# Sums of group 0's w2 made at the end of round one, y's splits ended there too, and last outputs sent by quarters

## The chip, the core and the metric

The kernel runs on one core of a Trainium2 chip. That core has a matmul engine (TensorE, PE in the rows; its weight loads are PEld), a vector engine (VectorE, DVE), a scalar engine (ScalarE, ACT), a general one (GpSimd, POOL) and a synchronising engine (SyncE, SP) that issues most of the DMAs. Each engine works through its own queue in order; semaphores order the engines among themselves. The metric is the device time of one execution in microseconds, as the median of several runs.

## The reference

Three stages follow each other, all in float32:

```python
a = softmax(scale * q_c @ k_full.T)         # 24 chunks of 32 queries; 8 memory keys + a window of 56
x = (a @ v_full) as [1536, 512]             # 1536 tokens
x = (sigmoid(x @ w_gate) * (x @ w_val)) @ w_out
p = probs / (probs.sum(-1) + 1e-9)
for e in range(4):                          # 4 experts, w1[e] is 512x1024, w2[e] 1024x512
    out += p[:, e:e+1] * (relu(x @ w1[e]) @ w2[e])
```

## The kernel before

The change lies wholly in the third stage, the mixture of four experts. Every float32 product is made of three matmuls: each operand is split into a high part (ACT, a cast) and a low part (DVE, the difference), and `mm3` (L181 to L183) multiplies high by high, high by low and low by high.

The four experts are cut into eight *groups* of 512 hidden columns. Tokens are cut into two halves of 768. **Round one** runs blocks 0 to 7, one group each, over the first half; **round two** runs blocks 8 to 15, the groups in reverse order, over the second half. Within a block, the product with w1 is made by a scheme of seven products instead of eight (products 1 to 7 into PSUM tiles `b`, `e` and `a`, in two units `u`, each 384 tokens wide), whose operands are sums and differences of quarters of w1 and of y, the stage's input. The product with w2 is plain in round one (`o_part`, PSUM tiles `d`, added into `acc` by `flush`, L819), and by the seven-product scheme again in round two, so that round two also needs sums of w2's quarters.

What is split or summed in round one is written to DRAM and read back in round two: `kept1` holds w1's seven operands of each group, `kept2` those of w2. `w1_prep(n)` loads and splits w1 of group n, `w2_prep(n)` splits w2 of group n into `w2` tiles and stores three operands (L296), `w2_sums(n)` makes the other four from the raw tiles in place (combinations L311, casts L316, low parts L322, store L324). The last group, 7, is not stored: round two begins with it. The raw w2 tiles come from a pool of two buffers, which are the two tiles of one group; `raw2_to` loads the next group (L223), and that load must wait until the buffers have been read for the last time. `yr` holds y, `yo` its seven split operands; `y_prep_late(1)` makes those of the second half, once block 7's last products have read the old ones.

The order of the work is written by hand. A block's preparations for the next one are lists of closures, `hooks`: `o_part` emits one of them after every three matmuls, the last two are kept back (`keep=2`) and emitted in the next block's first unit behind its first copy `s`. A second list, `thooks`, holds `w2_sums(n)` of blocks 1 to 7 and is emitted in the units. In block 0 the hooks were `w1_prep(1)` (9), `w2_sums(0)` (6) and `w2_prep(1)` (5). In block 7 they were `y_prep_late(1)` (8), of which two were left for round two (`hook(len(hooks))` behind product 6 of block 8). PSUM has eight banks, handed out in turn, so that a tile waits for the one allocated eight before it. `held` (L755) copies a product out of PSUM on ACT into `s`; `total` (L453 in round two) adds it to a later product on DVE.

In the last block, 15, the results of `stage` and `second` go to `st` tiles and are added into `acc` by DMAs of POOL (L524), except for the quarter (second half of the rows, second half of the columns), which DVE adds directly; then `acc` leaves in rows of 512 columns, three transfers from `second` (L518) and three from `c12` (L532).

Of the kernel before, what the change touches and what calls it, by code (L numbers as in the profile page):

```python
# [45 lines left out]
DH = DM // 2  # L46
# [26 lines left out]
def fused_kernel(ctx: ExitStack, tc: tile.TileContext, kq0, kq1, kvw, kvc, vl, w_g, w_v, w_o, w_1, w_2, probs, out):  # L73
# [144 lines left out]
    def raw2_to(n):  # L218
        for i in range(len(raw2s), min(n, len(groups))):
            raw2s[i] = []  # L220
            for fh in range(2):
                r = pools["raw2"].tile([128, 2, DM], F32, tag="raw2", name=f"raw2_{i}_{fh}")
                nc.sync.dma_start(out=r, in_=w_2[groups[i][0], groups[i][1], fh])  # L223
                raw2s[i].append(r)
# [56 lines left out]
    def w2_prep(n):  # L281
        def hi(u, fh):
            def do():
                raw2_to(n + 1)
                w = pools["wp2"].tile([128, 2, DM], F32R, tag="w2", name=f"w2_{n}_{u}_{fh}")
                ops2[n, u, fh] = w
                nc.scalar.copy(out=w[:, 0], in_=raw2s[n][fh][:, u])  # L287
            return do

        def lo(u, fh):  # L290
            def do():
                w = ops2[n, u, fh]
                nc.vector.tensor_tensor(out=w[:, 1], in0=raw2s[n][fh][:, u], in1=f32(w[:, 0]), op=ALU.subtract)  # L293
                if n < NSP:
                    for d in range(2) if fh else range(1):
                        nc.sync.dma_start(  # L296
                            out=kept2[n][:, d + 1 if fh else 0, u], in_=f32(w[:, :, d * DH:(d + 1) * DH]))
            return do


        h, l = ([fn(u, fh) for u in range(2) for fh in range(2)] for fn in (hi, lo))
        return [both(h[0], h[1], l[0]), both(h[2], l[1]), l[2], h[3], l[3]]

    def w2_sums(n):

        r0, r1 = raw2s[n]
        b = dict(b11=r0[:, :, :DH], b12=r0[:, :, DH:], b21=r1[:, :, :DH], b22=r1[:, :, DH:])
# [5 lines left out]
        def hi(m, x):  # L313
            def do():
                w = ops3[n][m] = wp.tile([128, 2, 2, DH], F32R, tag="w", name=f"w3_{n}_{m}")
                nc.scalar.copy(out=w[:, :, 0], in_=b[x])  # L316
            return do

        def lo(m, x):
# [10 lines left out]
            both(lo(7, "b12"), hi(6, "b22"), comb("b21", "b21", "b22", ALU.add)),  # L330
            both(lo(6, "b22"), hi(4, "b21")), both(lo(4, "b21"), lambda: raw2_to(n + 2))]

# [65 lines left out]

    def round_2(prev, hook, hooks, hp, sp, acc, held, product):

# [103 lines left out]
        firsts = {}  # L504

        def stage(n, th, tt, dh, ps):
            p, a, _ = of(n, th, tt, dh)
            if n == ends and (th, dh) == (1, 1):
                nc.vector.scalar_tensor_tensor(out=a, in0=ps[:, :DH], scalar=p, in1=a, op0=ALU.mult, op1=ALU.add)
                return  # L510
# [3 lines left out]
        def second(n, th, tt, dh, ps):  # L514
            p, a, t = of(n, th, tt, dh)
            if n == ends and (th, dh) == (1, 1):
                nc.vector.scalar_tensor_tensor(out=a, in0=ps[:, :DH], scalar=p, in1=a, op0=ALU.mult, op1=ALU.add)
                nc.sync.dma_start(out=out[(RT + t) * 128:(RT + t + 1) * 128], in_=acc[t])  # L518
                return
# [3 lines left out]
            if n > NR1:  # L523
                nc.gpsimd.dma_start(out=a, in_=st, accum_op=ALU.add)  # L524

        def c12(n, tt, ps):
# [3 lines left out]
            elif n == ends:  # L530
                nc.vector.scalar_tensor_tensor(out=a, in0=ps[:, :DH], scalar=p, in1=a, op0=ALU.mult, op1=ALU.add)
                nc.sync.dma_start(out=out[(RT + t) * 128:(RT + t + 1) * 128], in_=acc[t])  # L532
            else:
# [10 lines left out]
        for n in range(NR1, len(blocks)):  # L544
# [21 lines left out]
            s2 = held(b)  # L566
            hook(len(hooks))
            do("6")
# [6 lines left out]
            if late:  # L575
                left["4"](E2)
                load_w3(n, 6)
            lo(n, 0, 1, c11, True)
            product(n, 0, 5, b, False)
            total(b, s7, c22)  # L580
            hi(n, 0, 4, c22, True)
            do("5")
            lo(n, 0, 4, c22, True)
            product(n, 0, 4, e, False)
            total(e, s2, c21)
            hi(n, 0, 2, c21, True)
            do("3_2")
            lo(n, 0, 2, c21, True)
# [114 lines left out]

            if last:
                for tt in tts:
                    third(tt)
# [5 lines left out]
    def second_block():  # L712
# [45 lines left out]
        def unit(n, u, prev):  # L758
# [4 lines left out]
            if u == 0 and n:  # L763
                hook(len(hooks))
                thooks.extend(w2_sums(n))
            if u:
# [38 lines left out]
        def o_part(n, d, tt, u, first, last, cols):  # L805
            th, c = divmod(tt, RT // 2)
            c = slice(c * 128, (c + 1) * 128)
            for fh in range(2):
                h, w = H2[n, u, (fh, th)], ops2[n, u, fh]
                mm3(d[:, cols], h[:, 0, c], h[:, 1, c], w[:, 0, cols], w[:, 1, cols],  # L810
                    first and fh == 0, last and fh == 1)
                hook(keep=2)

# [12 lines left out]
        for n in range(NR1):  # L826
# [10 lines left out]
            if n == NR1 - 1:  # L837
                hooks.extend(y_prep_late(1))
            else:
                hooks.extend(w1_prep(n + 1))  # L840
                if n == 0:
                    hooks.extend(w2_sums(0))
                hooks.extend(w2_prep(n + 1))
            ds = {}
# [24 lines left out]
            part(5, 0)  # L869
            flushed(4)  # L870

            def prev(n=n, ds=ds):
                o_part(n, ds[5], 5, 1, False, True, ALL)
                flush(n, ds[5], 5, ALL)

        round_2(prev, hook, hooks, hp, sp, acc, held, product)
        pools["yo"].release()
# [432 lines left out]
```

## Time and profile before

| what | value |
|---|---|
| median of 3 runs | 855.52 us (854.46 to 857.11) |
| the profiled execution | 854.76 us, of which the span is 852.5 us |
| granted clock of TensorE, mean | 0.995 |
| busy: PE, PEld, DVE, ACT, POOL | 98%, 89%, 60%, 46%, 10% of the span |
| moved by DMA | 167.66 MB, mean 197 GB/s |

The span runs from the first to the last instruction on the chip; the profiled execution's own time is 2.3 us longer. PE's busy share counts matmuls whose ends are modelled and that overlap each other, so it does not say how well PE is used; where PE stood still is read from the waits. Round one starts at about 345 us, round two at about 605 us. In the chain of work that ended last, PE holds 93% of the span, DMA and DVE 2% each.

### The profile page before, as it was taken

What the parts mean: (1) busy time and instruction counts of PE and PEld (TensorE: products, weight loads), DVE (VectorE), ACT (ScalarE), POOL (GpSimd) and SP (SyncE); (2) the same over time, 40 slices, a digit from 0 to 9 for tenths busy, and PEclk for the clock granted to TensorE, in tenths of its full rate; (3) what the DMA queues carried; (4) which work ended last, traced back from release to release, by engine and by line L of the source; (5) the groups of instructions that cost most, each with busy time, mean ns of one, the idle gap of its engine ahead of it and who ended that gap; (6) DMA issues with size and microseconds to landing.
All of it is one profiled execution on the core that took longest, in us unless ns stands there. A gap on an engine that the chain in (4) does not pass through costs nothing.

```text
span 852.5 us, 13705 instructions
## 1 busy us (share of the span) xinstructions
PE 834.3 (98%) x5246; PEld 756.7 (89%) x5246; DVE 514.4 (60%) x963; ACT 392.7 (46%) x835; POOL 88.0 (10%) x101
## 2 busy tenths in 40 slices
PE   9999999999999999978999999999999999999997
PEld 6899998888888888867889989989899999999997
DVE  7754346432342238458997787788467556646756
ACT  5765354322332344525355445346255445545542
POOL 2311000000000000000000000000001343243232
PEclk9999999999999999998999999999999999999999
DMA  8974134121120004594977987730397999999974
GB/s 313 365 271 157 33 125 140 50 75 50 50 75 1 1 0 168 178 342 187 359 265 282 342 292 267 286 142 2 103 357 225 245 305 327 300 277 292 342 167 112
DMA packets 62338, 167.66 MB, mean 197 GB/s; under 512 B 6577, under 2 KB 27329, under 8 KB 62273
## 3 DMA queue, kind: packets, MB, share of 16 engines
q1 hardware_dynamic: 51008, 156.54, 51.1%
q0 software_dynamic: 11264, 10.25, 7.9%
q8 instruction: 41, 0.67, 0.3%
q14 instruction: 25, 0.20, 0.1%
HBM read 102.01 MB, written 54.53 MB: 184 GB/s over the span
## 4 chain that ended last, share of the span: by engine, by line
PE 93%; DMA 2%; DVE 2%; ACT 1%; issue 0%; SPq 0%; POOL 0%; ACTq 0%; DVEq 0%
PE b L181 5%; PE b L182 5%; PE b L183 5%; PE d L183 5%; PE d L182 5%; PE d L181 4%; PE pv L181 4%; PE pv L183 4%; PE pv L182 4%; PE pg L183 4%; PE pg L182 4%; PE pb L182 4%; PE pb L183 4%; PE pb L181 4%; PE pg L181 4%; PE B L183 3%
## 5 line engine op out<-in xcount | busy, mean ns | idle before, releaser
L524 POOL DMA_DIRECT2D acc<-st x60 | 52.4, 970 | 687.7 <-DVE st L522 682.7
L181 PE MATMUL b<-yo,w 128*128 128x384 f32 x256 | 87.9, 343 | 10.3 <-ACT s L755 9.0
L182 PE MATMUL b<-yo,w 128*128 128x384 f32 x256 | 86.8, 339 | 0.0
L183 PE MATMUL b<-yo,w 128*128 128x384 f32 x256 | 86.7, 339 | 0.0
L755 ACT COPY s<-b 128x384 f32<-128x384 f32 x64 | 30.6, 478 | 94.1 <-PE b L183 93.9
L181 PE MATMUL pv<-xs,w_v 128*128 128x384 f32 (+1 forms) x176 | 64.2, 365 | 0.0
L183 PE MATMUL pv<-xs,w_v 128*128 128x384 f32 (+1 forms) x176 | 61.8, 351 | 0.4 <-POOL w_v L161 0.4
L182 PE MATMUL pv<-xs,w_v 128*128 128x384 f32 (+1 forms) x176 | 61.5, 349 | 0.0
L181 PEld LDWEIGHTS b<-yo,w 128*128 128x128 f32 x256 | 48.4, 189 | 14.3 <-ACT s L755 11.6
L1052 ACT ACTIVATE sg<-pg 128x512 f32<-128x512 f32 x36 | 21.5, 598 | 84.2 <-PE pg L183 84.2
L183 PE MATMUL pg<-xs,w_g 128*128 128x512 f32 x144 | 56.0, 389 | 0.0
L182 PE MATMUL pg<-xs,w_g 128*128 128x512 f32 x144 | 56.0, 389 | 0.0
L181 PE MATMUL pb<-hl,w_o 128*128 128x512 f32 x144 | 56.0, 389 | 0.0
L182 PE MATMUL pb<-hl,w_o 128*128 128x512 f32 x144 | 56.0, 389 | 0.0
L183 PE MATMUL pb<-hl,w_o 128*128 128x512 f32 x144 | 56.0, 389 | 0.0
L181 PE MATMUL pg<-xs,w_g 128*128 128x512 f32 x144 | 56.0, 389 | 0.0
L120 DVE TENSOR_TENSOR hl<-g,hl 128x512 fp32r<-128x512 f32 x36 | 24.7, 690 | 48.5 <-ACT hl L119 48.5
L182 PEld LDWEIGHTS b<-yo,w 128*128 128x128 f32 x256 | 48.4, 189 | 1.0
L183 PEld LDWEIGHTS b<-yo,w 128*128 128x128 f32 x256 | 48.3, 189 | 0.0
L119 ACT CAST hl<-g 128x512 fp32r<-128x512 f32 x36 | 22.2, 623 | 54.8 <-PE pb L183 54.8
L181 PE MATMUL e<-yo,w 128*128 128x384 f32 x128 | 43.2, 338 | 0.2 <-ACT st L535 0.2
L293 DVE TENSOR_TENSOR w<-raw,w 128x512 fp32r<-128x512 f32 x32 | 21.2, 687 | 36.7 <-ACT w L287 28.4
(757 smaller groups left out, 2310.9 us busy)
## 6 DMA issues: line engine op xcount, KB each, us to landing
kept<-w SPq DMA_DIRECT2D x77, 512.0 KB, 6.8
w<-kept SPq DMA_DIRECT2D x49, 512.0 KB, 9.5
w_ring<-kept SPq DMA_DIRECT2D x38, 512.0 KB, 6.6
raw<-in_w_dram SPq DMA_DIRECT2D x32, 512.0 KB, 6.6
kept<-w SPq DMA_DIRECT2D x42, 256.0 KB, 6.8
acc<-st POOLq DMA_DIRECT2D x78, 128.0 KB, 5.3
kv<-in_kvc_dram SPq DMA_DIRECT2D x20, 483.0 KB, 5.9
raw<-in_w_v_dram SPq DMA_DIRECT2D x12, 512.0 KB, 6.7
```

Of the source, the lines that this page charges most:

```text
L119: nc.scalar.copy(out=hi, in_=src)
L120: nc.vector.tensor_tensor(out=lo, in0=src, in1=f32(hi), op=ALU.subtract)
L181: nc.tensor.matmul(out=ps, lhsT=w_hi, rhs=r_hi, start=first, stop=False, skip_group_check=more)
L182: nc.tensor.matmul(out=ps, lhsT=w_hi, rhs=r_lo, start=False, stop=False, skip_group_check=more)
L183: nc.tensor.matmul(out=ps, lhsT=w_lo, rhs=r_hi, start=False, stop=last, skip_group_check=more)
L293: nc.vector.tensor_tensor(out=w[:, 1], in0=raw2s[n][fh][:, u], in1=f32(w[:, 0]), op=ALU.subtract)
L524: nc.gpsimd.dma_start(out=a, in_=st, accum_op=ALU.add)
L755: nc.scalar.copy(out=s, in_=ps[:, :HT])
L1052: nc.scalar.activation(out=sg, in_=ps, func=AF.Sigmoid)
```

## The change

Five edits. `raw2_to(2)` is called behind the last low part of `w2_prep(0)`, so that group 1's raw w2 is loaded there. Block 0's hooks no longer hold `w2_sums(0)`. Instead `raw2_to` can load a ninth pair of tiles, `raw2_8`, which is group 0 once more; the load is called at the end of `w2_sums(7)`, and block 7's hooks are `y_prep_late(1)` and `w2_sums(0)` from those tiles, with `keep` 0, so that nothing is left for round two. The four operands of `w2_sums(0)` then come from the pool `rawp` instead of `wp`. In the first unit of each block of round two `lo` of a product stands behind the next `total`. In block 15 both column halves of the second half of the rows are added by DVE (no staging on ACT, no POOL DMA), and every output leaves by itself as 128 rows of 256 columns (`put_out`): those of the second half as soon as each is summed, those of the first columns of the first half (`late_out`, added by POOL) behind them, then the last three.

```diff
     def raw2_to(n):
-        for i in range(len(raw2s), min(n, len(groups))):
+        for i in range(len(raw2s), min(n, NR1 + 1)):
+            g = groups[i % NR1]
...
-                nc.sync.dma_start(out=r, in_=w_2[groups[i][0], groups[i][1], fh])
+                nc.sync.dma_start(out=r, in_=w_2[g[0], g[1], fh])
...
                 nc.vector.tensor_tensor(out=w[:, 1], in0=raw2s[n][fh][:, u], in1=f32(w[:, 0]), op=ALU.subtract)
+                if n == 0 and (u, fh) == (1, 1):
+                    raw2_to(2)
...
-    def w2_sums(n):
-
-        r0, r1 = raw2s[n]
+    def w2_sums(n, at, pool, tag):
+
+        r0, r1 = raw2s[at]
...
-                w = ops3[n][m] = wp.tile([128, 2, 2, DH], F32R, tag="w", name=f"w3_{n}_{m}")
+                w = ops3[n][m] = pool.tile([128, 2, 2, DH], F32R, tag=tag, name=f"w3_{n}_{m}")
...
-            both(lo(6, "b22"), hi(4, "b21")), both(lo(4, "b21"), lambda: raw2_to(n + 2))]
+            both(lo(6, "b22"), hi(4, "b21")), both(lo(4, "b21"), lambda: raw2_to(at + 2))]
...
+        def put_out(t, dh, a):
+            nc.sync.dma_start(out=out[(RT + t) * 128:(RT + t + 1) * 128, dh * DH:(dh + 1) * DH], in_=a)
+
         def stage(n, th, tt, dh, ps):
             p, a, _ = of(n, th, tt, dh)
-            if n == ends and (th, dh) == (1, 1):
+            if n == ends and th:
...
         def second(n, th, tt, dh, ps):
             p, a, t = of(n, th, tt, dh)
-            if n == ends and (th, dh) == (1, 1):
+            if n == ends and th:
                 nc.vector.scalar_tensor_tensor(out=a, in0=ps[:, :DH], scalar=p, in1=a, op0=ALU.mult, op1=ALU.add)
-                nc.sync.dma_start(out=out[(RT + t) * 128:(RT + t + 1) * 128], in_=acc[t])
+                put_out(t, dh, a)
                 return
...
+            if n == ends:
+                late_out.append((t, dh, a))
...
             s2 = held(b)
-            hook(len(hooks))
             do("6")
...
-            lo(n, 0, 1, c11, True)
             product(n, 0, 5, b, False)
             total(b, s7, c22)
             hi(n, 0, 4, c22, True)
+            lo(n, 0, 1, c11, True)
             do("5")
-            lo(n, 0, 4, c22, True)
             product(n, 0, 4, e, False)
             total(e, s2, c21)
             hi(n, 0, 2, c21, True)
+            lo(n, 0, 4, c22, True)
...
             if last:
+                for args in late_out:
+                    put_out(*args)
                 for tt in tts:
                     third(tt)
...
-                thooks.extend(w2_sums(n))
+                thooks.extend(w2_sums(n, n, wp, "w"))
...
-                hook(keep=2)
+                hook(keep=2 if n < NR1 - 1 else 0)
...
-                hooks.extend(y_prep_late(1))
+                hooks.extend(y_prep_late(1) + w2_sums(0, NR1, rawp, "raw"))
             else:
-                hooks.extend(w1_prep(n + 1))
-                if n == 0:
-                    hooks.extend(w2_sums(0))
-                hooks.extend(w2_prep(n + 1))
+                hooks.extend(w1_prep(n + 1) + w2_prep(n + 1))
...
+            if n == NR1 - 1:
+                hook(len(hooks))
```

PE's matmuls keep their order. The places that move are on SP and DVE. In the rows below `raw2_1_0` and `raw2_1_1` are the raw w2 tiles of group 1, `w3_0_5` and the like the summed operands of group 0.

SP in block 0, before:

```order
L215 DMA raw1_3_1_3547<-in_w_1_dram 128x1024
L324 DMA kept2_0_85<-w3_0_5_3556 128x1024
L324 DMA kept2_0_85<-w3_0_7_3564 128x1024
L324 DMA kept2_0_85<-w3_0_6_3573 128x1024
L324 DMA kept2_0_85<-w3_0_4_3581 128x1024
L223 DMA raw2_1_0_3589<-in_w_2_dram 128x1024
L223 DMA raw2_1_1_3591<-in_w_2_dram 128x1024
```

SP in block 0, now:

```order
L299 DMA kept2_0_85<-w2_0_0_1_3361 128x2x256 x2
L299 DMA kept2_0_85<-w2_0_1_0_3392 128x2x256
L224 DMA raw2_1_0_3444<-in_w_2_dram 128x1024
L224 DMA raw2_1_1_3446<-in_w_2_dram 128x1024
L299 DMA kept2_0_85<-w2_0_1_1_3399 128x2x256 x2
L266 DMA kept1_1_79<-w1_1_4_3481 128x1024
```

The load of `raw2_1` moved from behind the four stores of group 0's sums to the stores of group 0's splits, ahead of all seven `kept1` stores of group 1; the stores of the sums are gone from here.

DVE from the end of block 7 to the first sums of block 8, before (`yo3` to `yo6` are y operands, `d7_0` to `d7_5` the PSUM tiles that `flush` reads, `c0` and `c2` the sums of block 8):

```order
L230 TENSOR_TENSOR yo4_2866<-yr0_2859,yo4_2866 128x768
L819 SCALAR_TENSOR_TENSOR acc0_3316<-d7_0_5572,p_sb_75,acc0_3316 128x512
L819 SCALAR_TENSOR_TENSOR acc1_3317<-d7_1_5582,p_sb_75,acc1_3317 128x512
L819 SCALAR_TENSOR_TENSOR acc2_3318<-d7_2_5602,p_sb_75,acc2_3318 128x512
L819 SCALAR_TENSOR_TENSOR acc3_3319<-d7_3_5613,p_sb_75,acc3_3319 128x512
L819 SCALAR_TENSOR_TENSOR acc4_3320<-d7_4_5650,p_sb_75,acc4_3320 128x512
L819 SCALAR_TENSOR_TENSOR acc5_3321<-d7_5_5665,p_sb_75,acc5_3321 128x512
L230 TENSOR_TENSOR yo5_2867<-yr0_2859,yo5_2867 128x768
L230 TENSOR_TENSOR yo3_2868<-yr1_2860,yo3_2868 128x768
L453 TENSOR_TENSOR c0_5684<-a8_0_5731,s_5701 128x384
```

DVE from the same y split on, now (the flushes of `d7_1` to `d7_5`, left out here, and then the sums `c0` and `c2` follow):

```order
L231 TENSOR_TENSOR yo4_2866<-yr0_2859,yo4_2866 128x768
L231 TENSOR_TENSOR yo5_2867<-yr0_2859,yo5_2867 128x768
L231 TENSOR_TENSOR yo3_2868<-yr1_2860,yo3_2868 128x768
L314 TENSOR_TENSOR raw2_8_0_5552<-raw2_8_0_5552 128x2x256
L314 TENSOR_TENSOR raw2_8_0_5552<-raw2_8_1_5554,raw2_8_0_5552 128x2x256
L325 TENSOR_TENSOR w3_0_5_5614<-raw2_8_0_5552,w3_0_5_5614 128x2x256
L314 TENSOR_TENSOR raw2_8_1_5554<-raw2_8_0_5552,raw2_8_1_5554 128x2x256
L325 TENSOR_TENSOR w3_0_7_5622<-raw2_8_0_5552,w3_0_7_5622 128x2x256
L314 TENSOR_TENSOR raw2_8_1_5554<-raw2_8_1_5554 128x2x256
L830 SCALAR_TENSOR_TENSOR acc0_3316<-d7_0_5556,p_sb_75,acc0_3316 128x512
L325 TENSOR_TENSOR w3_0_6_5630<-raw2_8_1_5554,w3_0_6_5630 128x2x256
L325 TENSOR_TENSOR w3_0_4_5640<-raw2_8_1_5554,w3_0_4_5640 128x2x256
```

The two y splits moved from behind the sixth flush to before the first, and the eight instructions of `w2_sums(0)` stand around the first flush.

## Rows read from the trace of the kernel before

**Rows 1.** Waits of PE, 300 to 430 us: who waited for whom, total, times, longest.

```profile
PE b L181 <- ACT s L755: 9.0, 2, 8.3
```

**Rows 2.** Chain of work that ended last, 366 to 395 us: start, length, what.

```profile
375.45 0.94 SPq L223
376.44 9.26 DMA raw<-in_w_dram
...
386.24 0.61 ACT w L287
386.85 0.39 ACT s L755
387.28 0.69 PE b L181
```

**Rows 3.** Timeline of PE, first matmuls of blocks 1, 2, 3: start, length, what.

```profile
375.36 0.33 PE L181 MATMUL b<-yo,w 128*128 128x384 f32 x1
...
416.75 0.33 PE L181 MATMUL b<-yo,w 128*128 128x384 f32 x1
...
448.07 0.33 PE L181 MATMUL b<-yo,w 128*128 128x384 f32 x1
```

**Rows 4.** Stretch 385 to 390: busy PE, PEld, DVE, ACT, POOL; granted clock; DMA share, GB/s.

```profile
385.00:390.00 5.00, 2.72 (x8) 2.72 (x9) 4.89 (x8) 2.89 (x7) 0.00 (x0) 0.50 0.58 195
```

**Rows 5.** Timeline of DVE in block 0.

```profile
356.17 0.68 DVE L293 TENSOR_TENSOR w<-raw,w 128x512 fp32r<-128x512 f32 x1
...
368.65 0.69 DVE L311 TENSOR_TENSOR raw<-raw 128x512 f32<-128x512 f32 x1
```

**Rows 6.** Timeline at the seam, DVE, ACT and PE; in brackets idle time before, releaser.

```profile
590.87 0.68 DVE L322 TENSOR_TENSOR w<-raw,w 128x512 fp32r<-128x512 f32 x1
...
594.55 1.82 DVE L230 TENSOR_TENSOR yo<-yr,yo 128x768 fp32r<-128x768 f32 x2
...
606.06 0.48 ACT L755 COPY s<-b 128x384 f32<-128x384 f32 x1 [10.93 <-PE b L183]
...
608.44 0.76 DVE L819 SCALAR_TENSOR_TENSOR acc<-d,p_sb,acc 128x512 f32<-128x512 f32 x1 [4.10 <-PE d L183]
...
610.72 0.96 DVE L230 TENSOR_TENSOR yo<-yr,yo 128x768 fp32r<-128x768 f32 x1 [0.67 <-ACT yo L227]
...
611.60 0.55 DVE L453 TENSOR_TENSOR c<-a,s 128x384 f32<-128x384 f32 x1
...
612.09 0.34 PE L182 MATMUL e<-yo,w 128*128 128x384 f32 x1
...
612.26 0.34 PE L183 MATMUL e<-yo,w 128*128 128x384 f32 x1
...
613.28 0.55 DVE L453 TENSOR_TENSOR c<-b,s 128x384 f32<-128x384 f32 x1
...
613.98 0.41 PE L181 MATMUL b<-yo,w 128*128 128x384 f32 x1 [1.37 <-DVE c L453]
```

**Rows 7.** Line L223, the 16 loads of raw w2.

```profile
DMA to landing us min/median/max: 5.0/6.4/9.3
```

**Rows 8.** Timeline of the tail, DVE and SP's issues.

```profile
844.44 0.48 DVE L517 SCALAR_TENSOR_TENSOR acc<-B,p_sb,acc 128x256 f32<-128x256 f32 x1 [0.23 <-PE B L183]
...
846.60 0.48 DVE L531 SCALAR_TENSOR_TENSOR acc<-B,p_sb,acc 128x256 f32<-128x256 f32 x1 [0.23 <-PE B L183]
...
846.81 1.37 SPq L532 DMA_DIRECT2D out_dram<-acc  x3
```

**Rows 9.** Landing of outputs: line L532 (the last three), then L821 (round one's).

```profile
DMA to landing us min/median/max: 2.8/3.4/3.5
...
DMA to landing us min/median/max: 2.0/2.0/2.3
```

**Rows 10.** Stretches with `kept2` stores alone, then with POOL's additions; columns as in rows 4.

```profile
355.00:360.00 5.00, 5.00 (x28) 4.87 (x29) 3.52 (x8) 2.19 (x5) 0.00 (x0) 1.00 0.75 262
...
843.00:844.00 1.00, 1.00 (x10) 1.00 (x9) 0.97 (x3) 0.00 (x0) 1.00 (x2) 1.00 0.92 131
```

More of the change, by code (lines that the diff above doesn't have):

```diff
@@ L397, in emit, with round_2 @@
             todo.pop(0)()
-    def round_2(prev, hook, hooks, hp, sp, acc, held, product):
+    def round_2(prev, hp, sp, acc, held, product):
         h_op = [hp.tile([128, 2, HT], F32R, tag="h", name=f"h2_{i}") for i in range(8)]
@@ L524, in second @@
                 nc.gpsimd.dma_start(out=a, in_=st, accum_op=ALU.add)
+            if n == ends:
+                late_out.append((t, dh, a))
+        late_out = []
         def c12(n, tt, ps):
@@ L531, in c12 @@
                 nc.vector.scalar_tensor_tensor(out=a, in0=ps[:, :DH], scalar=p, in1=a, op0=ALU.mult, op1=ALU.add)
-                nc.sync.dma_start(out=out[(RT + t) * 128:(RT + t + 1) * 128], in_=acc[t])
+                put_out(t, 1, a)
             else:
@@ L874, in prev @@
                 flush(n, ds[5], 5, ALL)
-        round_2(prev, hook, hooks, hp, sp, acc, held, product)
+        round_2(prev, hp, sp, acc, held, product)
         pools["yo"].release()
```

## The prediction, made before the result was known

> **What bounds the kernel now.** The program is one long stream of matmuls, so I read first the waits of TensorE (PE): who made it stand still, and for how long. One entry stands out [rows 1]: 9.0 us in two waits behind ScalarE's copy `s` (L755), 8.3 us of it in one piece. That so little else is listed says that PE is the bound nearly everywhere, and that work taken from ACT or DVE beside the matmuls is worth nothing by itself. A gain must come from this wait, from the seam of the two rounds, or from the tail behind the last matmul.
>
> *The long wait.* The chain of waits [rows 2], read backward from PE at 387.28, goes to ACT's copy `s`, to ACT's cast of w2 of group 1 (L287), to the DMA that brings `raw2_1` (9.26 us), to its issue on SP at 375.45. It was issued so late because the pool of raw w2 tiles holds one group: group 1 can be loaded only when group 0's tiles have been read for the last time, by the `w2_sums(0)` that block 0 makes behind `w1_prep(1)`. ACT takes its queue in order, so `s`, which needs nothing of w2, stood behind the cast. Cost: the first matmuls of blocks 1, 2 and 3 start at 375.36, 416.75 and 448.07 [rows 3]. Block 1 took 41.39 us, block 2 31.32. The difference, 10.07 us, holds the wait and the slow stretch behind it: in 385 to 390 the granted clock was 0.50, the lower of the two levels (1.2 GHz), after PE had stood still for 8.3 us [rows 4].
>
> *The seam.* Between 596.37 (594.55 + 1.82) and 608.44 DVE has only flushes to do, and the one at 608.44 even waited 4.10 us for PE; yet two y splits were kept for round two [rows 6]. The last of them, at 610.72, holds the sum `c` of `a` until 611.60 and that of `b` until 613.28. Product 3, which adds to `b`, starts at 613.98, 1.72 us after the matmul before it, where neighbours (612.09, 612.26) are 0.17 apart. Loss: 1.55 us.
>
> *The tail.* The last sum on DVE starts at 846.60 and takes 0.48 [rows 8]; the span ends at 852.5.
>
> **The change, part by part.**
>
> *Block 0: w2_sums(0) leaves, raw2_1 is loaded early.* The load now stands behind the last w2 split of group 0, which ran at 356.17 to 356.85 [rows 5]. SP has only `kept2` writes before it, so both issues, of at most 0.94 each [rows 2], are out by about 358.8. Landing (from the issue's end) took 5.0 to 9.3 us in the 16 loads of this line [rows 7]: 363.8 to 368.1. It is needed when the hooks reach `w2_prep(1)`, where the sums began before: 368.65 [rows 5]. Even the slowest landing is half a microsecond early. From then on block 0 has the pattern of blocks 1 to 6, and behind block 1 no wait of PE for their casts is listed. The eight DVE and four ACT instructions and four `kept2` writes that leave ran beside matmuls: nothing by themselves. Term: -10.1 us; bounds 0 (the cast waits for something else) and -10.1.
>
> *Block 7: w2_sums(0) added, from a second load.* The two loads go out when `w2_sums(7)` is done, whose last `lo` starts at 590.87 [rows 6]; SP has nothing before them. With issues to 592.6 and 5.0 to 9.3 us for landing [rows 7] they are there at 597.6 to 601.9. On DVE come first two y splits of 0.95 (free at about 598.2), then four combinations and four `lo` at 0.69 [rows 5] and the five flushes at 0.76 [rows 6], less some overlap: 598.2 + 5.5 + 3.8, with 0.5 for waits on ACT's four casts, is 608.0. So the cover (DVE's idle time before 608.44) is just used up, and the first sum of round two, due near 610.6, keeps 2 us of slack. Flushes come up to 6 us later than now; the PSUM bank that the first of them frees is wanted eight tiles on, by product 2 of block 8 near 609.3, and the first flush is done by 604. Behind the new `kept2` writes on SP stand the outputs of round one, for which nobody waits, and the next w1 load, which goes out behind the sixth flush as before. With the slowest landing the chain ends near 611.7, and the sum `c` is as late as now. Term 0; bound +1.5.
>
> *Seam.* Nothing of y is left for round two, and `total(b)` stands before `lo(c11)`. Product 5 ends six steps of 0.17 and its own 0.34 before and after 612.26, so about 611.6; the sum of `b` takes 0.55 [rows 6] and is done by 612.25, when PE is still in product 4 (next start 612.43). Term: -1.55, bound -1.2. The same exchange of `lo` and `total` in the seven later blocks: no wait of PE there, so 0.
>
> *Tail.* Halves of block 15 that ACT staged and POOL added by three DMAs are now summed on DVE: three instructions of 0.48 more there, at a place where DVE waited for PE (0.23 even before the sum at 844.44 [rows 8]). So the last sums stay: 0, bound +0.4. The outputs go as twelve transfers of 128 KB, not six of 256 KB. Before, the last three were issued from 846.81 on in 1.37 us, 0.46 each, so that the last was out at 848.2 [rows 8]; it landed up to 3.5 us later, since all six came at once [rows 9]. After: behind the sum that ends at 844.92 seven issues follow, which at 0.46 each are out at 848.1, and at best at 847.5 (0.46 behind the end of the last sum, 847.08). A landing with nothing beside it took 2.0 [rows 9]. Term: from -2.2 (0.7 sooner, 1.5 shorter) to 0; I take -1.3, nearer the short landing, since issues 0.46 apart leave each 128 KB its time. That holds if rows of 1 KB go fast: the POOL additions, in such rows, moved 131 GB/s with the DMA engines 0.92 busy; the `kept2` writes, in such pieces too, 262 at 0.75 [rows 10], which is 349 at full use, or 0.37 us for 128 KB. Plain writes are like the second. At the first rate a quarter takes 1.0 us, seven of them behind 844.92 and up to two left from before end at 853.9, against 848.2 + 3.5 = 851.7 now: +2.2 is the far bound.
>
> The Trainium skill speaks against this last edit: DMA: Bandwidth & Descriptors, section "Bandwidth", asks for batches of a megabyte or more, and "Anatomy of one DMA" there gives each transfer a fixed 2.0 us plus its bytes at 436 GB/s. [...] By that formula, as an estimate, a quarter lands only 0.3 us sooner than a half, and the sum would be a microsecond smaller than mine.
>
> **Sum.** -10.1 - 1.55 - 1.3 = -12.95. The profiled execution took 854.76 us (its span of 852.5 and 2.3 around it); that gives 841.8. The median of the three runs, 855.52, is 0.76 above this execution, so I forecast a median of 842.6.
>
> **Rivals.**
> A. *Part of it comes back.* ACT waits for a load in another block long enough for PE to feel it, the chain in block 7 is late, or rows of 1 KB are slow. For it: DVE's cover in block 7 is just used up. Price 2 to 6 us: 844.6 to 848.6.
> B. *The stall stays*: the cast has a second cause, such as a w2 tile that is not free. Against it: seven tiles for four in use leave three free, and the chain shows the DMA alone. Result 855.52 - 1.55 - 1.3 = 852.7.
> C. *The stall moves to the seam, and the kernel is slower.* The same mechanism: `raw2_8` lands late, and ACT's `s` of block 8 (606.06 now [rows 6]) stands behind the four casts. These end some 3.5 us after landing (four combinations and a cast), so each microsecond past 602.5 costs PE one, and the slow clock 1.8 more. To lose 12.95 and 2.6 us besides, the load would have to land near 616, over 23 us after its issue; the slowest of 16 took 9.3 [rows 7]. Result about 858.
>
> **How the numbers follow.** Forecast 0.86, A 0.07, B 0.04, C 0.03. Two versions of this kernel can be told apart by about 0.3%, 2.6 us. Faster by more: forecast, A and half of B, 0.95; within: half of B, 0.02; slower: C, 0.03. Range: low 840.2 (tail at -2.2, and runs that differ by 1.5 us); high 846.4 (seam chain +1.5 with the tail at 0 or slow rows, or most of A).
>
> **What would show it.** In the profile after: no wait of PE on `s` near 380 and a granted clock of 1.00 all through round one; block 1 as long as block 2, 31.3 us; raw2_1 issued near 357 and landed before its cast is due. At the seam no gap over 0.3 us before product 3 of block 8, with DVE busy from 598 to 608. At the end the last output landing 2.0 to 2.5 us after its issue, and the end 5 us behind the last matmul, not 6. I am wrong if PE waits on `s` again in block 1 or block 8, or if raw2_1 still lands later than ACT wants it.

## The result

The changed kernel took 843.11 us, the median of four runs (841.22 to 843.22), beside 855.71 us for the kernel before on the same chip: a ratio of 0.985, with a 95% interval of 0.983 to 0.987. Forecast were 842.6 us, in a range of 840.2 to 846.4. So the kernel is 12.6 us faster, and the forecast is half a microsecond off.

The profiled execution took 843.08 us, with a span of 841.3. Cut at the first matmul of a block, the spans of the two profiled executions compare like this (in us; worked out from the starts of the first `b<-yo` matmuls in PE's timeline, as those in [rows 3]; block 8 begins at 604.74 and 596.71, block 9 at 632.51 and 622.89; the last column runs from the end of the last matmul, at 846.56 and 836.68, to the end of the span):

| kernel | up to block 0 | block 0 | block 1 | blocks 2 to 7 | block 8 | blocks 9 to 15 | behind |
|---|---|---|---|---|---|---|---|
| before | 344.62 | 30.74 | 41.39 | 187.99 | 27.77 | 214.05 | 5.94 |
| after | 346.71 | 30.73 | 31.33 | 187.94 | 26.18 | 213.79 | 4.62 |
| difference | +2.09 | 0 | -10.06 | -0.05 | -1.59 | -0.26 | -1.32 |

Three of the differences stand where the change works: block 1, block 8, and the stretch behind the last matmul. Together they are -12.97. The first one, +2.09, lies in the first 11 us of the program, which no edit touches; the last section comes back to it.

### The profile page after: what moved, and what is told of

Its sections match the earlier page's. It is cut to its first block, busy times and chain, and to the rows that moved or that the text cites. A ratio compares the mean times of both kernels' runs of the same rounds, so it can differ in the third digit from the quotient of the medians.

```text
span 841.3 us, 13728 instructions
## 1 busy us (share of the span) xinstructions
PE 834.4 (99%) x5246; PEld 756.6 (90%) x5246; DVE 513.6 (61%) x966; ACT 392.0 (47%) x832; POOL 84.7 (10%) x98
## 4 chain that ended last, share of the span: by engine, by line
PE 98%; ACT 1%; DMA 0%; DVE 0%; POOL 0%; issue 0%; ACTq 0%
PE b L181 5%; PE d L182 5%; PE d L183 5%; PE b L182 5%; PE b L183 5%; PE d L181 5%; PE pv L181 4%; PE pv L183 4%; PE pv L182 4%; PE pg L182 4%; PE pb L182 4%; PE pb L181 4%; PE pg L183 4%; PE pg L181 4%; PE pb L183 4%; PE B L183 3%
## 5 line engine op out<-in xcount | busy, mean ns | idle before, releaser
L530 POOL DMA_DIRECT2D acc<-st x57 | 49.3, 950 | 673.7 <-DVE st L528 673.2
L181 PE MATMUL e<-yo,w 128*128 128x384 f32 x128 | 43.2, 338 | 0.0
L182 PE MATMUL e<-yo,w 128*128 128x384 f32 x128 | 43.1, 337 | 0.0
```

Source lines behind the costliest of these rows:

```text
L181: nc.tensor.matmul(out=ps, lhsT=w_hi, rhs=r_hi, start=first, stop=False, skip_group_check=more)
L182: nc.tensor.matmul(out=ps, lhsT=w_hi, rhs=r_lo, start=False, stop=False, skip_group_check=more)
```

## The profile after

Waits of PE, over the whole span (who waited for whom: us in total, times, longest):

```profile
PE warm L933 <- DVE zero L1079: 1.1, 1, 1.1
PE b L181 <- ACT s L766: 0.7, 1, 0.7
PE pv L183 <- POOL w_v L161: 0.3, 1, 0.3
```

The 9.0 us of [rows 1] are gone. What is left behind `s` is one wait of 0.7 us in block 0, which was there before as the second of the two. The first matmuls of blocks 1, 2 and 3:

```profile
377.44 0.33 PE L181 MATMUL b<-yo,w 128*128 128x384 f32 x1
...
408.77 0.33 PE L181 MATMUL b<-yo,w 128*128 128x384 f32 x1
...
440.10 0.33 PE L181 MATMUL b<-yo,w 128*128 128x384 f32 x1
```

Block 1 now takes 31.33 us, as long as block 2 (31.33). The stretch of [rows 4] again (busy PE, PEld, DVE, ACT, POOL; granted clock; DMA share, GB/s):

```profile
385.00:390.00 5.00, 5.00 (x30) 5.00 (x29) 4.81 (x10) 3.40 (x7) 0.00 (x0) 1.00 0.17 71
```

PE worked all the time there and the granted clock read 1.00, not 0.50. The reason stands in the timelines, SP's first and then ACT's (start, length, what; in brackets idle time before it and the releaser):

```profile
358.36 1.14 SPq L224 DMA_DIRECT2D raw<-in_w_dram  x2
```

```profile
368.51 1.66 ACT L288 CAST w<-raw 128x512 fp32r<-128x512 f32 x3
378.76 0.48 ACT L766 COPY s<-b 128x384 f32<-128x384 f32 x1 [8.60 <-PE b L183]
```

The load of `raw2_1` went out at 358.36, where it had started at 375.45 [rows 2]; its casts ran at 368.51 without waiting, and `s` at 378.76 waited for PE, not PE for `s`.

The seam, on DVE and then on PE:

```profile
590.00 0.69 DVE L314 TENSOR_TENSOR raw<-raw 128x512 f32<-128x512 f32 x1
...
595.65 2.72 DVE L830 SCALAR_TENSOR_TENSOR acc<-d,p_sb,acc 128x512 f32<-128x512 f32 x4
600.40 0.75 DVE L830 SCALAR_TENSOR_TENSOR acc<-d,p_sb,acc 128x512 f32<-128x512 f32 x1 [2.04 <-PE d L183]
602.56 0.56 DVE L456 TENSOR_TENSOR c<-a,s 128x384 f32<-128x384 f32 x1 [1.40 <-PE a L183]
603.62 0.56 DVE L456 TENSOR_TENSOR c<-b,s 128x384 f32<-128x384 f32 x1 [0.51 <-PE b L183]
```

```profile
604.23 0.34 PE L183 MATMUL e<-yo,w 128*128 128x384 f32 x1
604.41 0.34 PE L181 MATMUL b<-yo,w 128*128 128x384 f32 x1
```

The second of these lines is product 3 of block 8. It starts 0.18 us behind the matmul before it; before, it was 1.72 [rows 6]. DVE makes the sums of group 0 from 590.00 on and is done with five flushes at 598.37 (595.65 + 2.72). Then it waits for PE again, 2.04 and 1.40 us: there is room left.

The tail: DVE's last sum, SP's issues, the landing of these twelve outputs (line L510), and a stretch in it:

```profile
836.72 0.48 DVE L541 SCALAR_TENSOR_TENSOR acc<-B,p_sb,acc 128x256 f32<-128x256 f32 x1 [0.23 <-PE B L183]
```

```profile
832.14 6.20 SPq L510 DMA_DIRECT2D out_dram<-acc  x12
```

```profile
DMA to landing us min/median/max: 1.7/1.8/1.8
```

```profile
837.00:838.00 1.00, 0.00 (x0) 0.00 (x0) 0.20 (x1) 0.00 (x0) 0.00 (x0) 1.00 0.80 268
```

SP issues twelve outputs in 6.20 us; its last issue starts at 837.94, 0.74 us after the end of the last sum (837.20), and ends at 838.34. Each quarter lands 1.7 to 1.8 us after the start of its issue, against 2.8 to 3.5 in [rows 9], which the profile counts in the same way.

## Experiments: the stall of block 1

**The stall put back.** In the changed kernel, `w2_sums(0)` goes back to block 0 and `raw2_1` is loaded behind it.

```diff
...
-                if n == 0 and (u, fh) == (1, 1):
-                    raw2_to(2)
...
-                hooks.extend(y_prep_late(1) + w2_sums(0, NR1, rawp, "raw"))
+                hooks.extend(y_prep_late(1))
             else:
-                hooks.extend(w1_prep(n + 1) + w2_prep(n + 1))
+                hooks.extend(w1_prep(n + 1))
+                if n == 0:
+                    hooks.extend(w2_sums(0, 0, wp, "w"))
+                hooks.extend(w2_prep(n + 1))
```

> The changed kernel with its first two edits taken back: w2_sums(0) is made in block 0 again and group 1's raw w2 is loaded behind it; seam, exchange and tail stay as changed, and nothing is left out of the computation. Theory (the late load of raw2_1 is the whole of the first gain): PE waits 8 to 9 us on s at the start of block 1 again, block 1 takes 41.4 us instead of 31.3, and the time is 843.1 + 10.1 = 853.2. Rival (block 0's sums themselves, or something else in the change, made part of the difference): block 1 takes clearly less than 41 us, or the time is not 10 us above 843.1.

Measured: 851.46 us (851.21 to 853.88), block 1 43.10 us in the profiled execution, the slowest of the five. Block 8 and the tail stay short (26.18 and 4.77). PE's wait, and the chain that led to it:

```profile
PE b L181 <- ACT s L764: 9.9, 2, 9.2
```

```profile
376.36 0.94 SPq L224
377.36 10.19 DMA raw<-in_w_dram
...
388.71 0.39 ACT s L764
389.14 0.69 PE b L181
```

It is the chain of [rows 2], with a load that took 10.19 us and not 9.26, and the price follows the load: 9.2 us of waiting, not 8.3. So the stall goes with these two edits and comes back with them. The size is not exact: the medians rose by 8.4 us, where the theory had 10.1, while block 1 of the profiled execution is 11.8 longer (43.10 for 31.33). How long the load took in the other four executions the record does not show.

**The kernel before, with the same work in another order.** Only the six hooks of `w2_sums(0)` change places with the nine of `w1_prep(1)`.

```diff
             else:
-                hooks.extend(w1_prep(n + 1))
                 if n == 0:
                     hooks.extend(w2_sums(0))
+                hooks.extend(w1_prep(n + 1))
                 hooks.extend(w2_prep(n + 1))
```

> The kernel before with one edit: in block 0 the six hooks of w2_sums(0) stand ahead of w1_prep(1) and not behind it, so that the raw w2 tiles are read for the last time earlier and raw2_1 is loaded earlier. The same work in the same block, nothing added or left out. Theory (only the late load costs): the wait of PE on s in block 1 goes, block 1 takes 31 to 32 us, 855.7 - 10.1 = 845.6, if the w1 splits do not come late in turn. Rival (block 0 has more work than its 30 us hide, wherever it stands): block 1 stays near 41 us, or the wait moves to w1's operands at the start of block 1, 850 to 856.

Measured: 845.13 us (844.87 to 846.75), beside 855.52 before, a ratio of 0.987 (0.985 to 0.989). SP's load of `raw2_1`:

```profile
369.32 1.92 SPq L223 DMA_DIRECT2D raw<-in_w_dram  x2
```

The load starts 22.47 us after block 0 (which began at 346.85), where it was 30.83 in the kernel before (375.45 - 344.62). Block 1 takes 31.37. Nothing was taken out of block 0: only the moment of the load counts. Most of what the change gains can be had by exchanging two lines, without a second load and without moving the sums into block 7. It leaves block 8 (27.77) as it was, and the tail (5.67) nearly so.

**The casts behind the first `s`.** In the kernel before, block 0 keeps back five hooks, and all casts of group 1's w2 then stand behind block 1's first `s` on ACT.

```diff
-                hook(keep=2)
+                hook(keep=5 if n == 0 else 2)
```

> The kernel before with one number changed: in block 0 five hooks are kept back for block 1 and not two, so that no cast of raw2_1 stands before the first copy s of block 1 on ACT. The load is as late as before. Theory (s waits only because ACT takes its queue in order): the first wait of PE goes from b behind s to a later place, where products that need w2 or the next s stand behind the casts, and is shorter: s runs at once, PE goes on for up to 6 us, 2 to 6 us saved, 850 to 854. Rival (the s copy is late for another reason): the wait of 8.3 us stays where it is, 855.7.

Measured: 854.63 us (853.83 to 855.30), a ratio of 0.998 (0.997 to 0.999): 0.9 us faster, where the theory had 2 to 6 and the rival nothing. ACT, then PE, then a later stretch (columns as above):

```profile
376.78 0.48 ACT L755 COPY s<-b 128x384 f32<-128x384 f32 x1 [2.80 <-PE b L183]
385.19 0.62 ACT L287 CAST w<-raw 128x512 fp32r<-128x512 f32 x1 [7.93 <-DMA raw<-in_w_dram]
```

```profile
380.87 0.34 PE L183 MATMUL a<-yo,w 128*128 128x384 f32 x1
388.51 0.69 PE L181 MATMUL e<-yo,w 128*128 128x384 f32 x1 [7.30 <-ACT s L755]
```

```profile
391.00:393.00 2.00, 2.00 (x8) 2.00 (x7) 1.77 (x4) 1.34 (x3) 0.00 (x0) 0.50 0.75 264
```

The first `s` ran at once, as the theory of ACT's order said, and PE went two products further. But there the next `s` stood behind the same casts. The wait became 1.0 us shorter (7.30 for 8.27), and the slow clock took it back: after the wait PE ran with matmuls 0.32 us apart for 5.8 us (388.51 to 394.3), where in the kernel before it was 3.2 us (387.28 to 390.5). In both stretches the granted clock read 0.50. At the normal spacing of 0.17 the same matmuls take half of that, so about 1 us more went there, and block 1 is as long as before (41.36 for 41.39). A stall's price is the wait and the slow stretch behind it, and the second part differs: block 1 less its wait and less the 31.33 us of an undisturbed block leaves 1.8 us before, 2.7 here, and 2.6 with the stall put back. A shorter wait can have the longer slow stretch. So block 1 of the profiled execution holds nothing of the 0.9 us, and where they come from is open.

## Experiment: how much room the sums have in block 7

Behind the sums of group 0, DVE gets eight additions more, in place on raw tiles that nobody reads again; all that the kernel puts out is computed as before.

```diff
+                def again():
+                    for g in range(8):
+                        nc.vector.tensor_tensor(out=raw2s[NR1][0], in0=raw2s[NR1][0], in1=raw2s[NR1][1], op=ALU.add)
-                hooks.extend(y_prep_late(1) + w2_sums(0, NR1, rawp, "raw"))
+                hooks.extend(y_prep_late(1) + w2_sums(0, NR1, rawp, "raw") + [again])
```

> The changed kernel with eight further additions of 128x1024 on DVE behind the sums of group 0 in block 7, on raw tiles that nobody reads any more; the outputs stay as they are. Each takes 1.1 to 2.1 us, 9 to 17 us in all. Theory (DVE's cover there is its idle time before the last flush, about 4 us in the trace of the changed kernel): the sixth flush and the first sums of block 8 are late, PE stands still 5 to 12 us at the start of round two, 848 to 857. Rival (there is much more room than that, since the flushes and sums can come late): no wait over 1 us, 843 to 844.

Measured: 848.76 us in one run. DVE's additions, then PE's waits:

```profile
594.13 10.03 DVE L851 TENSOR_TENSOR raw<-raw,raw 128x1024 f32<-128x1024 f32 x8
```

```profile
PE b L181 <- DVE c L456: 5.4, 1, 5.4
```

10.03 us of work cost PE a wait of 5.4, so 4.6 us of it were hidden. The chain of sums does end at PE, behind the sum `c`, as the prediction's part on block 7 had it; ACT's `s`, which rival C put there, is not what PE waited for. Block 8 became 34.01 us, 7.8 longer: 5.4 of waiting and again some 2.4 of slow clock. If each microsecond past the room counts in full, the room for more work at this place is 4.6 us, where the forecast counted on 2; this is one run with one amount of work.

## Experiments: the seam

**The two y splits left to round two again.**

```diff
...
-                hook(keep=2 if n < NR1 - 1 else 0)
+                hook(keep=2)
...
-                hooks.extend(y_prep_late(1) + w2_sums(0, NR1, rawp, "raw"))
+                yl = y_prep_late(1)
+                hooks.extend(yl[:6] + w2_sums(0, NR1, rawp, "raw") + yl[6:])
...
-            if n == NR1 - 1:
-                hook(len(hooks))
...
             s2 = held(b)
+            hook(len(hooks))
             do("6")
```

> The changed kernel with the last two y splits left to round two again, behind product 6 of block 8; the sums of group 0 stay in block 7. Theory (these two splits hold the sums c of block 8): product 3 of block 8 starts 1.5 us late behind c again, all else as changed: 843.1 + 1.5 = 844.6. Rival (the exchange of lo and total did it): no wait there, 843.1. Rival (the added sums on DVE push the splits further back): more than 2 us.

**`lo` before `total` again.** The splits stay in block 7; the lines of the first unit go back.

```diff
+            lo(n, 0, 1, c11, True)
             product(n, 0, 5, b, False)
             total(b, s7, c22)
             hi(n, 0, 4, c22, True)
-            lo(n, 0, 1, c11, True)
             do("5")
+            lo(n, 0, 4, c22, True)
             product(n, 0, 4, e, False)
             total(e, s2, c21)
             hi(n, 0, 2, c21, True)
-            lo(n, 0, 4, c22, True)
```

> The changed kernel with lo standing before total again in the first unit of round two's blocks; all else as changed. Theory (PE waits for neither): no change, 843.1, and no wait at product 3 of block 8. Rival (the exchange took away the half microsecond that PE stood still on ACT's st near 754 us): a wait of 0.3 to 0.5 us on e returns there, and c of b at block 8 comes up to 0.7 us later, 843.1 + 0.3 to 0.8.

Measured: 841.92 us (841.47 to 843.65) and 843.11 (842.42 to 843.77): neither can be told from the changed kernel by its time. Block 8 shows what each is worth: 26.57 us with the splits left to round two, 26.66 without the exchange, 26.18 with both edits, 27.77 with neither. So the 1.5 us that the theory of the first run gave to the splits alone did not come back. DVE and PE with the splits in round two:

```profile
600.86 0.96 DVE L231 TENSOR_TENSOR yo<-yr,yo 128x768 fp32r<-128x768 f32 x1 [0.67 <-ACT yo L228]
601.74 0.55 DVE L456 TENSOR_TENSOR c<-a,s 128x384 f32<-128x384 f32 x1
602.21 0.55 DVE L456 TENSOR_TENSOR c<-b,s 128x384 f32<-128x384 f32 x1
```

```profile
602.90 0.41 PE L181 MATMUL b<-yo,w 128*128 128x384 f32 x1 [0.16 <-ACT h L461]
```

DVE with `lo` first (its name in the rows is L468):

```profile
602.75 0.56 DVE L456 TENSOR_TENSOR c<-a,s 128x384 f32<-128x384 f32 x1 [1.40 <-PE a L183]
603.89 0.56 DVE L468 SCALAR_TENSOR_TENSOR h<-c,h 128x384 fp32r<-128x384 f32 x1 [0.59 <-ACT h L461]
604.37 0.55 DVE L456 TENSOR_TENSOR c<-b,s 128x384 f32<-128x384 f32 x1
```

The chain of the kernel before was split, sum of `a`, `lo`, sum of `b`. Either edit takes about 1.1 to 1.2 us out of it, and the second one then has only 0.4 to 0.5 left to take. The 1.59 belong to both together, not to the splits alone. The exchange has no part in the 0.26 us of blocks 9 to 15 either: without it they took 213.78.

## Experiments: the tail

The edit to the tail does two things: POOL's three additions near the end go, and the transfers become smaller. Three kernels part them.

**Outputs by halves, with POOL's additions** (the tail as before):

```diff
...
-            if n == ends and th:
+            if n == ends and (th, dh) == (1, 1):
...
-                put_out(t, dh, a)
+                nc.sync.dma_start(out=out[(RT + t) * 128:(RT + t + 1) * 128], in_=acc[t])
```

> The changed kernel with the outputs of block 15 sent by halves of 256 KB as before, one column half staged on ACT and added by POOL's DMA. Theory (smaller, earlier transfers land sooner): the time from the last matmul's end to the end of the span goes from 4.6 to 5.9 us, 843.1 + 1.3 = 844.4. Rival (the gain is an accident of one execution): it stays at 4.6 to 5.0.

**Outputs by halves, without the additions:**

```diff
-                put_out(t, dh, a)
+                if dh:
+                    nc.sync.dma_start(out=out[(RT + t) * 128:(RT + t + 1) * 128], in_=acc[t])
                 return
...
-                put_out(t, 1, a)
+                nc.sync.dma_start(out=out[(RT + t) * 128:(RT + t + 1) * 128], in_=acc[t])
```

> The changed kernel with its outputs of block 15 sent as six transfers of 256 KB, while both column halves of the second half of the rows are still summed on DVE, with no staging and no POOL addition for them. With u_tail (POOL additions and halves: 5.34 us from the last matmul to the end) and the changed kernel (neither: 4.62) it parts the tail edit in two. Theory 1 (the additions of POOL are what the outputs wait for): about 4.6 us. Theory 2 (the size of the transfers): about 5.3 us.

**Outputs by quarters, with the additions** (the same edit in `stage` and in `second`):

```diff
-            if n == ends and th:
+            if n == ends and (th, dh) == (1, 1):
...
```

> The changed kernel with the other half of the tail edit: one column half of the second half of the rows is staged on ACT and added by POOL again, and all outputs leave as quarters of 128 KB, those six behind the others' sums. Theory 1 (POOL's additions): 5.3 us or more from the last matmul to the end. Theory 2 (the size): about 4.6 us.

Measured, in us from the end of the last matmul to the end of the span:

| | halves of 256 KB | quarters of 128 KB |
|---|---|---|
| POOL adds | 5.34 (the changed kernel with the old tail); 5.67 to 5.94 (before, and the two kernels made from it) | 6.57 |
| DVE sums | 3.61 | 4.62 (after) |

The whole times are 842.63 us (842.14 to 843.35) for the old tail, 840.74 for halves without additions and 843.90 for quarters with them (one run each of the last two); they hold starts that differ by up to 2 us, so the tails are compared and not the times. Neither theory of the second kernel had 3.61; of the third, the theory of POOL's additions held.

What SP waited for ahead of its outputs, in the kernel before and then in the first of the three:

```profile
SPq L518 <- DMA acc<-st: 25.7, 3, 24.6
```

```profile
SPq L524 <- DMA acc<-st: 25.6, 1, 25.6
```

With the old tail, a stretch under POOL's additions and one behind them, and the landing of the last three outputs:

```profile
833.00:834.00 1.00, 1.00 (x10) 1.00 (x9) 0.61 (x2) 0.00 (x0) 0.00 (x0) 1.00 0.94 135
...
836.00:837.00 1.00, 0.00 (x0) 0.00 (x0) 0.00 (x0) 0.00 (x0) 0.00 (x0) 1.00 1.02 389
```

```profile
DMA to landing us min/median/max: 2.7/2.8/2.9
```

Halves without the additions, SP's last three issues with their landing, and a stretch:

```profile
834.30 1.77 SPq L541 DMA_DIRECT2D out_dram<-acc  x3
```

```profile
DMA to landing us min/median/max: 2.0/2.1/2.1
```

```profile
835.00:836.00 1.00, 0.19 (x2) 0.00 (x0) 0.48 (x1) 0.00 (x0) 0.00 (x0) 1.00 1.02 385
```

Quarters with the additions, SP's issues:

```profile
832.29 6.47 SPq L510 DMA_DIRECT2D out_dram<-acc  x12
```

With halves, an output of 512 columns needs both of its column halves summed. So with the old tail SP could issue the first one only when POOL's addition to it had landed, at 833.66, 1.1 us ahead of the end of the last matmul (834.76); without the additions it went at 832.30, 2.9 us ahead of it (835.19). The kernel before shows this wait three times. Until then the DMA engines were 0.94 busy with the additions at 135 GB/s, and nearly all of the outputs had to pass behind them, at 389 GB/s. Take the additions away and halves end after 3.61 us: 1.7 to 2.3 us gained. How much of that is SP's wait and how much the busy DMA engines, no run tells apart.

With quarters the gain is as large (6.57 to 4.62), by another way. There SP never waited for an addition. But three quarters fewer are ready early, so its queue of twelve starts 2.8 us ahead of the end of the last matmul and not 4.5 us (832.14 in the changed kernel), and its last issue ends 3.6 us behind it and not 1.7.

Quarters are a loss of 1.0 us against halves (4.62 against 3.61). SP's last issue starts 0.74 us after the last sum, where that of the last half follows at once (835.74, behind a sum that ends at 835.71). The landing is shorter by some 0.2 to 0.3 (1.8 against 2.0 to 2.1). These two explain half of the loss; the other half lies behind the last landing, where 1.5 us pass to the end of the span, against 1.0 with halves. Why, the rows do not show.

The Trainium skill's rule that the prediction weighed (DMA: Bandwidth & Descriptors, "Bandwidth": batches of a megabyte or more) points the right way here, though no run tries a megabyte: at equal work halves end sooner than quarters. The estimate of 0.3 us that the prediction worked out from "Anatomy of one DMA" is what these rows show for the difference between a quarter and a half. The formula as a whole, which that section gives for transfers issued by GpSimd, puts a half at 2.6 us as an estimate; these, issued by SP, landed in 2.0 to 2.1, and the measurement decides.

**A faster version.** The changed kernel with the extra two hooks of block 0 dropped and the three outputs of the first columns issued by ACT:

```diff
...
             fin0 = unit(n, 0, prev)
-            if n == 0:
-                hook(2)
...
                 for args in late_out:
-                    put_out(*args)
+                    put_out(*args, nc.scalar)
```

> The changed kernel with two small edits: block 0's extra emission of two hooks between its units is dropped, so that the casts of w2 do not stand ahead of s there, and the outputs of the first columns (late_out) are issued by ACT beside SP's. Theory: the 0.7 us wait of PE on s in block 0 goes, and SP's queue in the tail is three issues of about 0.5 us shorter, so the last output is out 0 to 1 us sooner: 841.8 to 843.1. Rival (the last three outputs are bound by the last sums and by their landing, not by SP's queue): the tail stays at 4.6 us behind the last matmul and only the 0.7 goes; or the hooks that come later make a new wait, 843 to 845.

Measured: 840.19 us (839.64 to 841.85), a ratio to the kernel before of 0.981 (0.979 to 0.984). PE's waits, and the two queues in the tail:

```profile
PE b L181 <- ACT s L766: 0.2, 1, 0.2
```

```profile
830.54 5.42 SPq L510 DMA_DIRECT2D out_dram<-acc  x9
```

```profile
829.74 1.36 ACTq L510 DMA_DIRECT2D out_dram<-acc  x3
```

Block 0 took 30.22 us, 0.5 less. The tail took 3.42, 1.2 less than after, which is more than the upper end of the theory: with nine issues SP is out at 835.96, 0.37 us behind the last sum. So SP's queue held up the tail with quarters, by 0.7 us; most of the rest of the 1.2 lies behind the last landing (1.1 us to the end of the span, not 1.5). The Trainium skill (DMA: Bandwidth & Descriptors, section "Issuing engines are not separate DMA queues") says that a second issuing engine saves nothing but the time of issuing; here that time held up the last output, and saving it is worth having. Halves without additions and with the hooks dropped were not tried.

**Both once more, on one chip.**

> The changed kernel once more, unchanged. Its profiled execution began block 0 at 346.7 us, where three others began at 344.5 to 344.8, with matmuls of the first 10 us taking 1.5 to 1.8 times as long. Theory (this differs from execution to execution and belongs to no edit): times from about 841 to 843.5 us, in steps of one or two microseconds, and a start of either kind. Rival (the start of this kernel is slower in itself): all at 843, block 0 at 346.7 again.

> The kernel of the run best once more, beside the changed kernel on the same chip. Its two edits gave 0.5 us (block 0) and 1.2 us (tail) in the trace. Theory (the rest of the 2.9 us between their medians was the start): 1.2 to 2.2 us below the changed kernel. Rival: 2.9 us again.

Measured: 841.92 us (840.88 to 842.47) for the changed kernel and 840.27 (839.56 to 841.50) for the faster version: 1.65 apart, as the trace has it (0.5 + 1.2). The kernel before had 856.04 beside them.

## Why the prediction was right, step by step

- **Block 0 and block 1: -10.1 forecast, -10.06 measured.** The mechanism is the one named: the load was early, ACT's casts did not wait, the slow clock went too. Rival B (a second cause of the stall) fell with the result; the exchange of two lists of hooks in the kernel before shows that the moment of the load is all of it. Landing took 3.3 to 6.9 us in the 18 loads of this line, counted, as in [rows 7], from the start of the issue; the prediction counted it from the end, which made its latest landing too late and changed nothing.
- **Block 7: 0 forecast, 0 measured** (blocks 2 to 7: 187.94 for 187.99). The size of the room was wrong: 2 us forecast, 4.6 shown. The sums and five flushes took 8.4 us (590.00 to 598.37), not the 9.8 of the forecast, whose figures take off nothing for the overlap between neighbours and add a wait for casts. (Its 592.6 for the end of the issues does not follow either: two issues of 0.94 behind a `lo` that ends at 591.55 give 593.4.) Rival C had the right place and another chain: with too much work PE waited behind the sum `c`, not behind `s`.
- **Seam: -1.55 forecast, -1.59 measured.** The sum was right, its cause was half told. The prediction said that the splits hold both sums and gave the loss to them; either edit alone brings 1.1 to 1.2.
- **The exchange in the other blocks: 0 forecast, 0 measured.** The 0.26 us between the two profiled executions in blocks 9 to 15 is not the change's: the two kernels made from the kernel before have no exchange and took 213.78 there.
- **Tail: -1.3 forecast, -1.32 measured, and for the wrong reason.** The times of issue were right: nothing sooner, the last issue ends 1.66 us behind the last matmul and before 1.62. So was the shorter landing, by 1.7 us in the last output (1.8 for 3.5). But the prediction ascribed it to 128 KB pieces that are issued 0.46 us apart, and treated the end of POOL's additions as costing nothing and bringing nothing. The runs show otherwise: halves without the additions land in 2.0 to 2.1, so the size of the pieces has only 0.2 to 0.3 of the 1.7. The end of the additions brings 1.7 to 2.3 us of the tail, and the quarters take 1.0 back. Two terms that were not seen, of opposite sign, add up to the one that was written; that the sum fits is luck. The row was there: the one with 131 GB/s at 0.92 busy [rows 10] was read as a price of narrow rows, and not as what the outputs had to wait for.
- **From the execution to the median.** The three terms are right to 0.05 us in their sum (-12.95 and -12.97); the forecast of the median is 0.5 off in one set of runs and 0.7 the other way in the second (841.92). The profiled execution took 843.08 where the sum gave 841.8: 2.1 us more at the start, less 0.3 in the other blocks and 0.5 outside the span (1.8 us, before 2.3). The start differs from execution to execution by as much, as the last section shows.

## What to carry to other kernels

When an engine that works in order stands still behind a cast, ask when the load it waits for was issued and what freed its buffer; moving the last reader of the buffer forward was worth 10.4 us here, with no work added or left out. Price a stall as the wait plus the slow stretch that follows it. Take an edit that does two things apart before you credit one of them: here the tail gained by the transfers that disappeared, and lost by the ones that were cut smaller.

## What the runs showed of the hardware that was not expected

The same kernel starts in more than one way. In 14 profiled executions block 0 began at 344.5 to 346.9 us, and no edit touches what is ahead of it. PE's warming matmuls and the first products show where it comes from; first the execution of after, then that of the kernel with the old splits:

```profile
3.98 0.53 PE L933 MATMUL warm<-zero 128*128 128x384 bf16 x1
...
7.15 1.76 PE L933 MATMUL warm<-zero 128*128 128x384 bf16 x5
8.84 1.30 PE L951 MATMUL s<-kv 128*32 128x112 f32 x24
```

```profile
6.01 0.97 PE L933 MATMUL warm<-zero 128*128 128x384 bf16 x5
6.92 0.78 PE L951 MATMUL s<-kv 128*32 128x112 f32 x24
```

Five warming matmuls took 1.76 us in one and 0.97 in the other, and 24 products `s` 1.30 and 0.78. In after, all up to about 10 us ran in this way; in the other kernel nothing after 4.6 us did; in still others it ended at about 6. The granted clock reads 1.00 in all of these stretches, also in the first 4.5 us, where every execution is slow (ten warming matmuls in 3.38 us). These matmuls stand about 0.32 us apart in the slow stretches, as in the rows above where the granted clock read 0.50, and 0.16 in the fast ones. So by the durations the engine was at its lower level there, and in the first microseconds the record can't be used for it. The Trainium skill (TensorE: Matmul & The Clock Gate, in its part on the clock gate) says that the moment of the rise differs from run to run; these rows agree, and it is worth up to 2.3 us here, nearly as much as two versions of this kernel must differ by to be told apart. The changed kernel's second profile has five warming matmuls of 0.97 at 6.79, so it is no property of the kernel.

That profile still began block 0 at 346.04, as a smaller part of the spread has another source: ACT waited there 0.8 us for a load of `w_v` at about 17 us, and 0.9 in the execution with the stall put back. The kernel before and the profile of after show no such wait.
